# The narrow product's copy and lower part given out as scheduler steps, and a tile's first fifth-block product moved behind the fifth of the seven products

## The chip, the cores and the metric

One NeuronCore of a Trainium2 chip runs the program; the other cores are idle. The metric is the device time of one execution in microseconds (us). A kernel is run several times, and medians are compared. Times from the profile are from one profiled execution.

## What is computed

A layer with two residual parts over 4096 tokens of 640 channels. The first part is a spectral mixer: layer norm with a modulation from `c`, a two-dimensional FFT over the tokens, a complex two-layer MLP in four blocks of 160 channels with a soft shrink, and the inverse FFT. The second is a SwiGLU feed-forward network (FFN) with 1728 hidden channels. The change lies in the second.

```python
mod = (_silu(c) @ w_mod).reshape(c.shape[0], 6, 1, -1)
sa, ca, ga, sb, cb, gb = (mod[:, 0], mod[:, 1], mod[:, 2], mod[:, 3], mod[:, 4], mod[:, 5])
h = _layernorm(x, axis=-1) * (1 + ca) + sa
x = x + ga * _A_ref(h, A_w1, A_b1, A_w2, A_b2)
h = _layernorm(x, axis=-1) * (1 + cb) + sb
x = x + gb * _B_ref(h, B_w_gate, B_w_up, B_w_down)
...
g = _silu(x @ w_gate)
u = x @ w_up
return (g * u) @ w_down
```

All data is fp32. `_B_ref` is the FFN; `x` has 4096 rows of 640, `w_gate` and `w_up` are 640 by 1728, `w_down` is 1728 by 640.

## The kernel before

**Numbers.** Every fp32 operand is split in a high part (rounded to the type fp32r, which TensorE multiplies) and a low part (the rest). A product is three matmuls: high weight by high activation, high weight by low activation, low weight by high activation. In the code these are three lines next to each other, such as L1996, L1997, L1998.

**Tiles.** The FFN takes the tokens in six tiles. Tiles 0 and 1 have 512 tokens and use the plain form (`plain`). Tiles 2 to 5 have two halves of 384 tokens and use a form with seven products of half-size blocks in place of eight (`seven`, L1961): the 640 input channels are four blocks of 128, on which the seven products B11, B21, T3, T2, T4, T1 and B22 work, and a fifth block, which is multiplied in the ordinary way (`fifth`, three matmuls at L2007 to L2009). Each of the seven is six matmuls. The weights B are columns of the weight tile `wb`, the weights T are sums of them in `wt`. The eight activation operands of a tile, `h_0` to `h_7`, come from DRAM (`hs`) by two DMAs of SyncE's (SP's) queue each (`load_h`, L1808); `h_3` is the fifth block.

**Blocks of hidden channels.** 1728 channels are 13.5 blocks of 128. The first index `n` of `seven` is the block: a gate block and an up block of weights come in turn, `g0, u0, s, g1, u1, ...`. The entry `s` is the narrow remainder of 64 gate and 64 up columns, done after the first two blocks: inline in `plain` for tiles 0 and 1, by `rest` (L2125, matmuls L2160) for tiles 2 to 5, where it has two pieces, `a` = 0 and 1. What follows the matmuls of a narrow product is `mix_rem` (L1884): ScalarE (ACT) takes the silu of the gate rows (L1887), VectorE (DVE) multiplies by the up rows (L1888), ACT copies the result to the high part (L1889), DVE subtracts it for the low part (L1890). The result `a13` is read by the last down product of the tile.

**Banks.** The seven products accumulate in four banks of PSUM (the `1` in `pw_0_1` is the bank of that product). `keep` (L2015) copies a bank to SBUF on ACT (`s_x`, `s_v`, `s_y`, `s_z`), after which PE goes on to accumulate in the same bank, so that the second use of bank 0, for T2, waits for `s_x`. `summed` (L2022) adds bank and copy on DVE and gives the bank free. `lefts` makes the seven left factors `L_j` of the down product from the results: multiplications and differences on GpSimd (POOL, L2056 and L2067), high parts on ACT (L2072), low parts on DVE (L2076).

**What sets the order.** PE's stream is written by hand. Work of the other engines is of two kinds. Inline work is issued where it stands, so that it has its place in its engine's queue at that point of PE's stream. The rest are chains of steps (`Chain`, `Step`), each with an engine, an estimated cost, the keys it depends on, the key it gives and the buffers that it uses and frees. Between matmuls, `slot` moves a planner's clock on and issues the steps whose engines are free by the estimates, chains of the list `tails` first. `quiet` keeps steps off ACT just before a `keep`, `until` issues steps until a key is there, `hold` and `take` get a buffer. Each engine, and SP's queue of DMAs, works through its own queue in order, and SP's DMA waits for the one eight DMAs earlier. So the planner's estimates fix an order, and a change of one step's kind or cost can move those that come after it: residual rows (`cr`, `x`, stored as `x2d`, L1603 to L1662), transposes (`pt`), the second transform of the mixer for later rows (`py`, L1636), weights (`prep_w`: high part on ACT at L1383, low part on DVE at L1390), weights of the down product (`wq`, L1565). The down products' results are `pc` and `pe` (L2293, L2336).

Of the kernel before, what the change touches and what calls it, by code (L numbers as in the profile page):

```python
# [8 lines left out]
AF = mybir.ActivationFunctionType  # L9
OP = mybir.AluOpType  # L10
# [163 lines left out]
def body(tc, x, w1, b1, w2, b2, wg, wu, wd, c, wm, k_fa, k_tb, k_tx, k_bm, k_bx, k_ga, k_ge, k_id, out, dbg=None):  # L174
    nc = tc.nc
    pe, act, dve, pool = nc.tensor, nc.scalar, nc.vector, nc.gpsimd
    mm = pe.matmul

    def f32(ap):
        return ap.bitcast(F32)  # L180
# [21 lines left out]
    with ExitStack() as top:  # L202
# [836 lines left out]
        with ExitStack() as ff:  # L1039
# [203 lines left out]
            def core(e, n, at=0.0):  # L1243
                start = max(free[e], now[0] + 0.17, at)
                free[e] = start + n
                return free[e] + LAT
# [634 lines left out]
                done["fv"] = 5.0  # L1881
                return pg

            def mix_rem(pg, n, a13, nm, tag="sg"):  # L1884
                hold(tag)
                sg = take(tag, [P, n], F32, 4, f"sgr{nm}")
                act.activation(sg[0:64], pg[0:64, :n], AF.Silu)  # L1887
                dve.tensor_tensor(sg[0:64], pg[64:128, :n], sg[0:64], op=OP.mult)  # L1888
                act.activation(a13[0:64, :], sg[0:64], AF.Copy)  # L1889
                dve.tensor_tensor(a13[64:128, :], sg[0:64], f32(a13[0:64, :]), op=OP.subtract)  # L1890
                x = core("A", n / 960 + 0.09)
                x = core("V", n / 960 + 0.15, x)
                x = core("A", n / 960 + 0.09, x)
                x = core("V", n / 960 + 0.15, x)
                room[tag].append(x)
                return x


            def plain(t, n):
                k, p = WG[n]  # L1900
                wb = wbs[t, n]
                pg = []
                for f in range(1 if k == "s" else 2):
                    if (t, n) == (0, 0):
                        if f == 0:
                            hold("p1")
                            b2 = first_g()
                            slot(7.4)
                        pg.append((b2[f], "p1" if f else None))
                    else:  # L1910
                        b, q = any_bank(f"pg{t}_{n}_{f}")
                        pg.append((b, q))
                        for kk in range(5):
                            if t:
                                until(("ht", t, kk))
                                wait_pe(done["ht", t, kk])
                            hh, hl = (ht[t, kk][:, i] for i in range(2))
                            wh, wl = (wb[:, i, kk, 128 * f:128 * f + 128] for i in range(2))
                            mm(b, wh, hh, start=(kk == 0), stop=False)  # L1919
                            mm(b, wh, hl, start=False, stop=False)  # L1920
                            mm(b, wl, hh, start=False, stop=(kk == 4))  # L1921
                            if n == NW - 1 and f == 1:
                                room[f"h{HT0[kk]}"].append(now[0] + 0.9)
                            slot(0.68)
                    if k == "s":
                        hold("rb0")
                        a13 = take("rb0", [P, 512], F32R, 1, f"a13_{t}")
                        acts[t, 13] = (a13, a13)
                        x = done["act", t, 13] = mix_rem(b, 512, a13, f"{t}")
                    else:  # L1930
                        x = finish0(t, n, f, pg[f][0])
                    if pg[f][1]:
                        room[pg[f][1]].append(x)
# [27 lines left out]
            def seven(t, n, last):  # L1961
# [41 lines left out]
                def fifth(q, half, f):  # L2003
                    need_h(3)
                    AK = hb[t, 3]
                    c = slice(P * f, P * f + P)
                    mm(bk[q], wb[:, 0, 4, c], AK[:, half, 0], start=False, stop=False, skip_group_check=True)  # L2007
                    mm(bk[q], wb[:, 0, 4, c], AK[:, half, 1], start=False, stop=False, skip_group_check=True)  # L2008
                    mm(bk[q], wb[:, 1, 4, c], AK[:, half, 0], start=False, stop=True, skip_group_check=True)  # L2009
                    go(3)  # L2010

                def keep(q, nm):
                    hold("s")
                    s = take("s", [P, N], F32, 10, f"s{t}_{n}_{nm}")
                    act.activation(s, bk[q], AF.Copy)  # L2015
                    return s, core("A", ca_)
# [79 lines left out]
                def rel(q, at):  # L2096
                    room[f"p{q}"].append(at)
# [8 lines left out]
                s1 = keep(0, "x")  # L2106
                quiet[0] = now[0] + 5 * m3
                prod(1, 1, "B21", True)
                fifth(1, 0, 0)
                rel(1, summed(0, 0, 1, s1))  # L2110
                need_wt(0)
                prod(3, 6, "T3", True)
                s7 = keep(3, "v")
# [7 lines left out]
                prod(0, 4, "T1")  # L2121
                room[wtags[t, n, 1]].append(now[0] + 0.2)
                sz = keep(0, "z")
                fifth(3, 1, 0)
                rel(3, summed(1, 0, 3, sy))  # L2125
                quiet[0] = now[0] + 5 * m3
# [10 lines left out]
            def rest(t, n):  # L2137
                N = P * TL[t][1]
                wb = wbs[t, n]
                A11, A12, A22, AK, S1 = (hb[t, j] for j in range(5))  # L2140
                for key in wb_keys(t, n):
                    until(key)
                    wait_pe(done[key])
                for a in range(2):
                    b, q = any_bank(f"pr{t}_{a}")
                    b = b[:, :N]
                    seq = []
                    for kp in range(2):
                        c = slice(0, P)
                        w1_ = [wb[:, hl, kp, c] for hl in range(2)]  # L2150
                        if a == 0:
                            w2_ = [wb[:, hl, 2 + kp, c] for hl in range(2)]
                        else:
                            w2_ = [wb[:, hl, kp, P:256] for hl in range(2)]
                        for l, w in (((A11, S1)[a], w1_), ((A12, A22)[a], w2_)):
                            seq += [(w[0], l[:, kp, 0]), (w[0], l[:, kp, 1]), (w[1], l[:, kp, 0])]
                    w = [wb[:, hl, 4, 0:P] for hl in range(2)]
                    seq += [(w[0], AK[:, a, 0]), (w[0], AK[:, a, 1]), (w[1], AK[:, a, 0])]
                    for i, (l, m) in enumerate(seq):
                        mm(b, l, m, start=(i == 0), stop=(i == len(seq) - 1))  # L2160
                        if i % 5 == 4:
                            slot((N + 32) / 2400 * 5)
                    hold("s")
                    a13 = take("s", [P, N], F32R, 10, f"a13_{t}_{a}")
                    acts.setdefault((t, 13), {})[a] = a13
                    x = done["act", t, 13, a] = mix_rem(b, N, a13, f"{t}_{a}", "s")
                    room[q].append(x)

            def down(t, pp):
# [311 lines left out]
```

## Time and profile before

| what | value |
|---|---|
| time, three runs | 1432.89, 1424.74, 1430.14 us |
| median of the three | 1430.14 us |
| the profiled execution's own time | 1433.04 us |
| its span in the trace | 1431.2 us |
| mean granted TensorE clock | 0.995 |
| the FFN's part of the span | from about 317 us to the end |

The profile gives for each engine the busy time, and for groups of instructions what ended the idle time before them (the releaser). An instruction that waits for several things is put down to the one that came last. In a timeline row stand the start, the duration, the engine, the line, the operation and, in brackets, the idle time before it with the releaser; `xN` at the end is a row of N instructions alike.

### The profile page before, as it was taken

The page shows a single profiled execution, that of the slowest core. Times are in us where ns is not written, and L with a number is a line of the kernel's source. Part 1 is how long each engine was busy: PE and PEld are TensorE (multiplying, and loading weights), DVE is VectorE, ACT ScalarE, POOL GpSimd, SP SyncE. Part 2 cuts the span into 40 slices and gives each one's busy share as a digit, 9 for nine tenths or more (in the row PEclk, how much of TensorE's full clock was granted, in tenths as well). Part 3 has the DMA queues.
Part 4 walks back from the last instruction along what each step waited for, and adds up shares of the span by engine and source line. Part 5 has one row for each costly group of instructions (what it writes and reads, how often), then busy time and mean ns, then how long its engine had stood idle before and what let it go on. Part 6 is the DMA issues. An engine that isn't in the chain of part 4 may idle for free.

```text
span 1431.2 us, 23776 instructions
## 1 busy us (share of the span) xinstructions
PE 1392.4 (97%) x8410; PEld 1313.5 (92%) x8410; DVE 1055.1 (74%) x1863; ACT 762.7 (53%) x1542; POOL 595.5 (42%) x681
## 2 busy tenths in 40 slices
PE   6899999999999999999999999999999999999999
PEld 2599999967888888899999999999999999999998
DVE  8979888879987797738787669787667557365654
ACT  6879999736555556435463446445355325152441
POOL 5600200036767586325455426456433325052241
PEclk9999999989999999999999999999999999999999
DMA  9866556556889988898868998888988566955634
GB/s 361 319 221 199 164 184 197 188 201 210 314 290 317 344 301 306 290 353 307 307 206 296 343 348 280 270 276 293 373 304 296 185 216 246 365 189 198 217 124 147
DMA packets 170872, 377.34 MB, mean 264 GB/s; under 512 B 22177, under 2 KB 81633, under 8 KB 168738
## 3 DMA queue, kind: packets, MB, share of 16 engines
q1 hardware_dynamic: 161650, 359.28, 72.9%
q0 software_dynamic: 6800, 13.93, 3.0%
q10 hardware_dynamic: 2304, 2.62, 0.5%
q8 instruction: 66, 1.08, 0.3%
q14 instruction: 52, 0.43, 0.1%
HBM read 269.48 MB, written 96.80 MB: 256 GB/s over the span
## 4 chain that ended last, share of the span: by engine, by line
PE 65%; issue 9%; DVE 9%; DMA 7%; ACT 5%; POOL 3%; SPq 1%; POOLq 0%; DVEq 0%; ACTq 0%
PE pc L2293 8%; PE pw L1996 7%; PE pw L1998 7%; PE pw L1997 7%; PE pe L2293 6%; PE pd L2209 5%; PE pg L1920 3%; PE pg L1919 3%; PE pg L1921 3%; PE pw L2007 2%; PE pw L2009 2%; PE pw L2008 2%; DMA h<-hs 2%; PE py L1636 1%; DVE wb L1390 1%
## 5 line engine op out<-in xcount | busy, mean ns | idle before, releaser
L1390 DVE TENSOR_TENSOR wb<-r,wb 128x768 fp32r<-128x768 f32 (+3 forms) x170 | 158.8, 947 | 14.3 <-ACT wb L1383 13.7
L2056 POOL TENSOR_TENSOR sg<-s_x,sg 128x384 f32<-128x384 f32 x24 | 30.3, 1261 | 278.9 <-DVE s_x L2022 278.9
L1996 PE MATMUL pw<-h,wt 128*128 128x384 f32 x412 | 139.8, 339 | 3.8 <-ACT s_x L2015 2.9
L1998 PE MATMUL pw<-h,wt 128*128 128x384 f32 x412 | 138.3, 336 | 0.0
L1997 PE MATMUL pw<-h,wt 128*128 128x384 f32 x412 | 138.1, 335 | 0.0
L2293 PE MATMUL pc<-wq,L 128*128 128x320 f32 x846 | 132.8, 310 | 2.5 <-DVE s_v L2022 1.7
L1383 ACT ACTIVATE wb<-r 128x768 fp32r<-128x768 f32 (+3 forms) x168 | 104.2, 638 | 53.3 <-PE pw L2009 38.8
L2293 PEld LDWEIGHTS pc<-wq,L 128*128 128x128 f32 x846 | 126.3, 188 | 3.3 <-DVE s_v L2022 2.2
L2015 ACT ACTIVATE s_x<-pw 128x384 f32<-128x384 f32 x52 | 25.5, 490 | 190.6 <-PE pw L1998 188.4
L2076 DVE TENSOR_TENSOR L<-sg,L 128x384 fp32r<-128x384 f32 x144 | 101.2, 720 | 27.8 <-ACT L L2072 26.8
L1996 PE MATMUL pw<-h,wb 128*128 128x384 f32 x312 | 104.9, 336 | 0.0
L1997 PE MATMUL pw<-h,wb 128*128 128x384 f32 x312 | 104.4, 335 | 0.0
L1998 PE MATMUL pw<-h,wb 128*128 128x384 f32 x312 | 104.3, 334 | 0.0
L1919 PE MATMUL pg<-ht,wb 128*128 128x512 f32 x260 | 102.1, 393 | 0.0
L1920 PE MATMUL pg<-ht,wb 128*128 128x512 f32 x260 | 101.3, 390 | 0.0
L1921 PE MATMUL pg<-ht,wb 128*128 128x512 f32 x260 | 101.3, 390 | 0.0
L2293 PE MATMUL pe<-wq,L 128*128 128x320 f32 x648 | 101.0, 309 | 0.0
L2209 PE MATMUL pd<-wq,a 128*128 128x320 f32 x632 | 97.0, 310 | 0.0
L2293 PEld LDWEIGHTS pe<-wq,L 128*128 128x128 f32 x648 | 96.5, 188 | 0.0
L2067 POOL TENSOR_TENSOR sg<-sg,sg 128x384 f32<-128x384 f32 x72 | 88.3, 1227 | 18.7 <-DVE L L2076 15.5
L2209 PEld LDWEIGHTS pd<-wq,a 128*128 128x128 f32 x632 | 93.4, 188 | 0.5
L2250 DVE TENSOR_TENSOR x<-x,pc 128x320 f32<-128x320 f32 x144 | 68.2, 483 | 31.5 <-PE pc L2293 31.2
(317 smaller groups left out, 3865.4 us busy)
## 6 DMA issues: line engine op xcount, KB each, us to landing
wq<-wqd SPq DMA_DIRECT2D x83, 640.0 KB, 5.3
wt<-td SPq DMA_DIRECT2D x103, 512.0 KB, 4.8
hs<-ho SPq DMA_DIRECT2D x52, 512.0 KB, 5.9
h<-hs SPq DMA_DIRECT2D x32, 768.0 KB, 7.7
td<-wt SPq DMA_DIRECT2D x25, 512.0 KB, 6.4
r<-in_B_w_gate_dram SPq DMA_DIRECT2D x24, 384.0 KB, 4.8
r<-in_B_w_up_dram SPq DMA_DIRECT2D x24, 384.0 KB, 4.1
xx<-tt SPq DMA_DIRECT2D x56, 160.0 KB, 3.3
```

The source lines that it names most:

```text
L1383: def high(ks, e=slice(0, c), copy=lambda o, i: act.activation(o, i, AF.Copy)):
L1390: dve.tensor_tensor(wbs[t, n][:, 1, ks, e], raw[t, n][:, ks, e], f32(wbs[t, n][:, 0, ks, e]), op=OP.subtract)
L1919: mm(b, wh, hh, start=(kk == 0), stop=False)
L1920: mm(b, wh, hl, start=False, stop=False)
L1921: mm(b, wl, hh, start=False, stop=(kk == 4))
L1996: mm(b, w(0, kp), a[:, kp, 0], start=start and kp == 0, stop=False, skip_group_check=not start)
L1997: mm(b, w(0, kp), a[:, kp, 1], start=False, stop=False, skip_group_check=not start)
L1998: mm(b, w(1, kp), a[:, kp, 0], start=False, stop=kp == 1, skip_group_check=not start)
L2067: pool.tensor_tensor(o, x, y, op=op)
L2076: dve.tensor_tensor(o[:, 1], raws[j], f32(o[:, 0]), op=OP.subtract)
L2209: mm(b[:, :320], l, m, start=start and i == 0, stop=stop and i == len(s) - 1)
L2293: mm(o[:, :320], ls[q][:, x, k], w[:, q, y], start=start and q == 0 and n == 0, stop=q == 1 and n == 2, skip_group_check=not start)
```

## The change

Two edits. First, in `mix_rem` the ACT copy and the DVE subtraction are no longer issued inline behind the multiplication. They become a chain of two steps in `tails`, with the key of the finished part passed in. The planner books the silu and the multiplication only, the function returns the end of the multiplication, and with that the product's PSUM bank is noted as free (in `rest` through `room[q]`); the buffer of `sgr` is freed by the second step. This concerns ten narrow products: one in each of tiles 0 and 1, two in each of tiles 2 to 5. Second, in `seven`, for the first block alone (`n == 0`, one place in each of tiles 2 to 5), the first fifth-block product and the addition that frees its bank move from behind B21 to behind T1 and the copy `s_z`: four products, or 24 matmuls, later.

```diff
@@ -1881,18 +1881,18 @@
                 done["fv"] = 5.0
                 return pg
 
-            def mix_rem(pg, n, a13, nm, tag="sg"):
+            def mix_rem(pg, n, a13, key, nm, tag="sg"):
                 hold(tag)
                 sg = take(tag, [P, n], F32, 4, f"sgr{nm}")
                 act.activation(sg[0:64], pg[0:64, :n], AF.Silu)
                 dve.tensor_tensor(sg[0:64], pg[64:128, :n], sg[0:64], op=OP.mult)
-                act.activation(a13[0:64, :], sg[0:64], AF.Copy)
-                dve.tensor_tensor(a13[64:128, :], sg[0:64], f32(a13[0:64, :]), op=OP.subtract)
                 x = core("A", n / 960 + 0.09)
                 x = core("V", n / 960 + 0.15, x)
-                x = core("A", n / 960 + 0.09, x)
-                x = core("V", n / 960 + 0.15, x)
-                room[tag].append(x)
+                done["mul", key] = x
+                tails.append(Chain([
+                    Step("A", n / 960 + 0.12, lambda: act.activation(a13[0:64, :], sg[0:64], AF.Copy), (("mul", key),), ("ah", key)),
+                    Step("V", n / 960 + 0.22, lambda: dve.tensor_tensor(a13[64:128, :], sg[0:64], f32(a13[0:64, :]), op=OP.subtract),
+                         (("ah", key),), key, free=(tag,))]))
                 return x
 
 
@@ -1926,7 +1926,7 @@
                         hold("rb0")
                         a13 = take("rb0", [P, 512], F32R, 1, f"a13_{t}")
                         acts[t, 13] = (a13, a13)
-                        x = done["act", t, 13] = mix_rem(b, 512, a13, f"{t}")
+                        x = mix_rem(b, 512, a13, ("act", t, 13), f"{t}")
                     else:
                         x = finish0(t, n, f, pg[f][0])
                     if pg[f][1]:
@@ -2106,8 +2106,9 @@
                 s1 = keep(0, "x")
                 quiet[0] = now[0] + 5 * m3
                 prod(1, 1, "B21", True)
-                fifth(1, 0, 0)
-                rel(1, summed(0, 0, 1, s1))
+                if n:
+                    fifth(1, 0, 0)
+                    rel(1, summed(0, 0, 1, s1))
                 need_wt(0)
                 prod(3, 6, "T3", True)
                 s7 = keep(3, "v")
@@ -2121,6 +2122,9 @@
                 prod(0, 4, "T1")
                 room[wtags[t, n, 1]].append(now[0] + 0.2)
                 sz = keep(0, "z")
+                if not n:
+                    fifth(1, 0, 0)
+                    rel(1, summed(0, 0, 1, s1))
                 fifth(3, 1, 0)
                 rel(3, summed(1, 0, 3, sy))
                 quiet[0] = now[0] + 5 * m3
@@ -2163,7 +2167,7 @@
                     hold("s")
                     a13 = take("s", [P, N], F32R, 10, f"a13_{t}_{a}")
                     acts.setdefault((t, 13), {})[a] = a13
-                    x = done["act", t, 13, a] = mix_rem(b, N, a13, f"{t}_{a}", "s")
+                    x = mix_rem(b, N, a13, ("act", t, 13, a), f"{t}_{a}", "s")
                     room[q].append(x)
 
             def down(t, pp):
```

The numbers of lines behind L2125 grow by 4. No instruction is added or removed. All engines' orders are the same up to the narrow product of tile 0, and differ in many places after it. Three places follow.

ACT in tile 3, from the first narrow piece (`pr_0`, result `a_3_0`) to the second (`pr_1`, `a_3_1`) and the copy `s_3_x` of the next block's first bank. Before:

```order
L1887 ACTIVATE sgr_0_9855<-pr_0_9825 64x384
L1889 ACTIVATE a_3_0_9854<-sgr_0_9855 64x384
L2072 ACTIVATE L_0_7_9882<-s_1_d 128x384
L2072 ACTIVATE L_0_2_9890<-sg_0_01_9672 128x384
L2072 ACTIVATE L_0_4_9893<-sg_0_11_9679 128x384
L1887 ACTIVATE sgr_1_9897<-pr_1_9860 64x384
L1889 ACTIVATE a_3_1_9896<-sgr_1_9897 64x384
L2015 ACTIVATE s_3_x<-pw_3_0_9902 128x384
L1383 ACTIVATE wb_4_9931<-r_4_9733 128x2x128
```

After:

```order
L1887 ACTIVATE sgr_0_9854<-pr_0_9814 64x384
L2072 ACTIVATE L_0_2_9863<-sg_0_01_9668 128x384
L2072 ACTIVATE L_0_4_9872<-sg_0_11_9673 128x384
L1893 ACTIVATE a_3_0_9853<-sgr_0_9854 64x384
L1383 ACTIVATE wb_3_9823<-r_3_9423 128x768
L1887 ACTIVATE sgr_1_9888<-pr_1_9857 64x384
L2072 ACTIVATE L_0_5_9897<-sg_0_10_9650 128x384
L1383 ACTIVATE wb_4_9903<-r_4_9706 128x2x128
L2015 ACTIVATE s_3_x<-pw_3_0_9892 128x384
L1893 ACTIVATE a_3_1_9887<-sgr_1_9888 64x384
```

The second narrow copy, which stood between the second silu and `s_3_x`, now stands behind `s_3_x`; the left factor `L_0_5` and a copy of the weights `wb_4` have come ahead of `s_3_x`, and the high part of the second piece of `wb_3` between the two silus.

DVE at the same place. Before:

```order
L1390 TENSOR_TENSOR wb_3_9835<-r_3_9423,wb_3_9835 128x2x128
L1390 TENSOR_TENSOR wb_3_9835<-r_3_9423,wb_3_9835 128x768
L1888 TENSOR_TENSOR sgr_0_9855<-pr_0_9825,sgr_0_9855 64x384
L1890 TENSOR_TENSOR a_3_0_9854<-sgr_0_9855,a_3_0_9854 64x384
L2076 TENSOR_TENSOR L_0_7_9882<-s_1_d,L_0_7_9882 128x384
L2076 TENSOR_TENSOR L_0_2_9890<-sg_0_01_9672,L_0_2_9890 128x384
L1888 TENSOR_TENSOR sgr_1_9897<-pr_1_9860,sgr_1_9897 64x384
L1890 TENSOR_TENSOR a_3_1_9896<-sgr_1_9897,a_3_1_9896 64x384
```

After:

```order
L1888 TENSOR_TENSOR sgr_0_9854<-pr_0_9814,sgr_0_9854 64x384
L2076 TENSOR_TENSOR L_0_2_9863<-sg_0_01_9668,L_0_2_9863 128x384
L2076 TENSOR_TENSOR L_0_4_9872<-sg_0_11_9673,L_0_4_9872 128x384
L1390 TENSOR_TENSOR wb_3_9823<-r_3_9423,wb_3_9823 128x2x128
L1888 TENSOR_TENSOR sgr_1_9888<-pr_1_9857,sgr_1_9888 64x384
L1390 TENSOR_TENSOR wb_3_9823<-r_3_9423,wb_3_9823 128x768
L1894 TENSOR_TENSOR a_3_0_9853<-sgr_0_9854,a_3_0_9853 64x384
```

The low parts of the next block's weights, `wb_3`, stood ahead of both narrow multiplications; now the second piece (128x768) stands behind the second multiplication.

SP in tile 4, from the loads of `wq` to those of `h_7` and `h_3` for its first `seven`. Before:

```order
L1565 DMA wq_2_0_11868<-wqt 128x1280
L1565 DMA wq_2_-1_11893<-wqt 128x1280
L1565 DMA wq_0_1_11913<-wqd 128x1280
L1808 DMA h_4_11927<-hs 128x1536
L1565 DMA wq_0_2_11932<-wqd 128x1280
L1808 DMA h_7_11943<-hs 128x1536
L1808 DMA h_3_11960<-hs 128x1536
L1744 DMA hs<-ho_1_0_11724 128x2x512
```

After:

```order
L1808 DMA h_2_11802<-hs 128x1536
L1565 DMA wq_2_-1_11824<-wqt 128x1280
L1607 DMA cr_11838<-s 128x640
L1662 DMA x2d<-x_11182 128x640
L1565 DMA wq_0_1_11864<-wqd 128x1280
L1808 DMA h_4_11886<-hs 128x1536
L1565 DMA wq_0_2_11891<-wqd 128x1280
L1662 DMA x2d<-x_11273 128x640
L1603 DMA x_11938<-in_A_x_dram 128x640
L1607 DMA cr_11954<-s 128x640
L1808 DMA h_7_11976<-hs 128x1536
L1808 DMA h_3_11998<-hs 128x1536
```

Two stores of rows, a load of a row and two loads of `cr` have come ahead of `h_7` and `h_3`. The row load (`x_11938`) waits, among other things, for the landing of the first of these stores.

## The prediction

> **What bounds the kernel now.** The page's head, with the busy time of each engine, and two stretches of the view of windows (us, then the busy time and instructions of PE, PEld, DVE, ACT and POOL, the granted TensorE clock, the DMA share, GB/s):
>
> ```profile
> span 1431.2 us, 23776 instructions
> PE 1392.4 (97%) x8410; PEld 1313.5 (92%) x8410; DVE 1055.1 (74%) x1863; ACT 762.7 (53%) x1542; POOL 595.5 (42%) x681
> ...
> 1030.00:1235.00 205.00, 203.41 (x1250) 202.40 (x1249) 128.49 (x234) 81.40 (x176) 66.01 (x63) 1.00 0.76 267
> 295.00:300.00 5.00, 4.80 (x13) 2.60 (x12) 4.89 (x8) 0.88 (x2) 0.31 (x1) 0.50 0.48 169
> ```
>
> TensorE sets the time, at the full clock (1.00) in the FFN's stretch; the other stretch lies before the FFN. The change neither adds nor removes a matmul, so it can only act on the moments in which PE waits. The view of waits, for PE in the FFN (317 us to the end), names these (engine, line, what it waited for: us in total, times, longest):
>
> ```profile
> PE pw L1996 <- ACT s_x L2015: 2.9, 3, 1.6
> PE py L1636 <- DVE chl L1626: 2.0, 2, 1.1
> PE pc L2293 <- DVE s_v L2022: 1.7, 2, 0.9
> PE py L1636 <- ACT a L1955: 1.6, 1, 1.6
> PE pw L2007 <- DMA h<-hs: 1.5, 2, 1.3
> PE pt L1699 <- ACT xn L1667: 1.2, 2, 0.8
> PE pw L1996 <- ACT s_v L2015: 0.8, 1, 0.8
> PE pc L2293 <- DMA wq<-wqd: 0.8, 1, 0.8
> PE pe L2336 <- DMA wq<-wqt: 0.4, 1, 0.4
> PE pt L1699 <- ACT h L1703: 0.2, 1, 0.2
> PE pt L1852 <- DVE xn L2379: 0.2, 1, 0.2
> ```
>
> They add up to 13.3 us, 0.9% of the span: the most that any reordering can bring. Two of the rows are what the change touches: 2.9 us on s_x, the copy of the first product's bank, and 1.5 us on h, the fifth block's activations. The other 8.9 us are at places that the edit doesn't name.
>
> **The narrow product's wait, in tile 3.** Rows of ACT, DVE, POOL and PE from the timeline (start, duration, engine, line; idle time before and its releaser in brackets):
>
> ```profile
> 856.83 1.02 POOL L2056 TENSOR_TENSOR sg<-s_v,sg 128x384 f32<-128x384 f32 x1
> 857.06 1.12 PE L2160 MATMUL pr<-h,wb 128*128 128x384 f32 x5
> 857.17 1.08 DVE L1890 TENSOR_TENSOR a<-sgr,a 64x384 fp32r<-64x384 f32 x1 [0.59 <-ACT a L1889]
> 858.02 0.33 PE L1996 MATMUL pw<-h,wb 128*128 128x384 f32 x1
> 858.31 0.47 ACT L1887 ACTIVATE sgr<-pr 64x384 f32<-64x384 f32 x1
> 859.06 0.33 PE L1996 MATMUL pw<-h,wb 128*128 128x384 f32 x1
> 860.03 1.36 DVE L2076 TENSOR_TENSOR L<-sg,L 128x384 fp32r<-128x384 f32 x1
> 861.31 0.55 DVE L1888 TENSOR_TENSOR sgr<-pr,sgr 64x384 f32<-64x384 f32 x1
> 861.90 0.52 ACT L1889 ACTIVATE a<-sgr 64x384 fp32r<-64x384 f32 x1 [3.12 <-DVE sgr L1888]
> 862.33 0.47 ACT L2015 ACTIVATE s_x<-pw 128x384 f32<-128x384 f32 x1
> 862.45 0.57 DVE L1890 TENSOR_TENSOR a<-sgr,a 64x384 fp32r<-64x384 f32 x1 [0.59 <-ACT a L1889]
> 862.85 0.45 PE L1996 MATMUL pw<-h,wt 128*128 128x384 f32 x1 [1.02 <-ACT s_x L2015]
> 867.38 0.95 DVE L1390 TENSOR_TENSOR wb<-r,wb 128x768 fp32r<-128x768 f32 x1
> ```
>
> ACT stood still 3.12 us before the narrow copy (L1889), because the multiplication (L1888) started only at 861.31, behind left factors on DVE. The copy of the first product's bank, s_x, was behind it in ACT's order, and PE needed that bank again. So the wait hangs on one instruction placed inline. The change takes it from that place, at ten places in all. The two first rows of the next fence are the same wait in tile 2 (651 to 657 us) and in tile 4 (1068 to 1073 us); the third row groups the low part at all ten (ns: min, median, max):
>
> ```profile
> PE pw L1996 <- ACT s_x L2015: 1.6, 1, 1.6
> ...
> PE pw L1996 <- ACT s_x L2015: 0.3, 1, 0.3
> ...
> L1890 DVE TENSOR_TENSOR a<-sgr,a x10: 552/742/1193, 343.9 to 1263.0; 64x384 fp32r<-64x384 f32 x8, 64x512 fp32r<-64x512 f32 x2
> ```
>
> **Its cost, step by step.** Removed: 1.6 in tile 2, 1.0 in tile 3, 0.3 in tile 4. But the order of the changed program shows something new in tile 3: on DVE, the second piece of the next weights' low part (128x768, 0.95 us in the row at 867.38) now stands behind the second multiplication, and that waits for the narrow product's end, which I call E. Ready is it at about E + 0.13 (858.31 less the end 858.18 of PE's row at 857.06) + 0.47 (silu) + 0.55 + 0.95 and some 0.1 of handovers, E + 2.2. PE gets to B21's first matmul with the low weights after the six of B11 (858.02 to 859.06: 1.04 us, 0.173 each) and two more, at E + 1.4. So PE waits 0.8 us there, and of tile 3's 1.0 remain 0.2. On ACT, s_x has the left factor L_5 and a weight copy ahead of it now; PE uses the bank again 15 matmuls after B11, 2.6 us, and 0.8 more with that wait, which covers both. Sum: -1.6 - 1.0 + 0.8 - 0.3 = -2.1 us. Bounds: -2.9, if the low weights come in time; 0, if each stall only goes over to the next item in ACT's and DVE's orders. I take -2.1, since of the three places the order shows a new wait at one.
>
> The copies and low parts themselves (10 of 0.52 us, 10 of 0.55 to 1.19) are done later, beside matmuls on engines that are busy 53% and 74% of the span; only the last down products of a tile read them, tens of us later. Were that cover gone, the longest pair would be 0.52 + 1.19 = 1.7 us at one place. Cost taken: 0.
>
> **The fifth block's product.** PE in tiles 3 and 4 (timeline), the piece before it from the chain that ended last, SP's issues of h_7 and h_3, and landing times grouped by issue (KB, median us), for h between 1000 and 1045 us and for the row store between 590 and 630:
>
> ```profile
> 833.77 0.44 PE L2007 MATMUL pw<-h,wb 128*128 128x384 f32 x1 [0.21 <-DMA h<-hs]
> ...
> 1040.93 0.34 PE L1998 MATMUL pw<-h,wb 128*128 128x384 f32 x1
> 1042.61 0.44 PE L2007 MATMUL pw<-h,wb 128*128 128x384 f32 x1 [1.34 <-DMA h<-hs]
> ...
> 1031.38 11.19 DMA h<-hs
> ...
> 1025.11 0.34 SPq L1565 DMA_DIRECT2D wq_-1_11893<-wqt  x1
> 1030.76 1.05 SPq L1808 DMA_DIRECT2D h<-hs  x2
> ...
> h<-hs SPq DMA_DIRECT2D x8, 768.0 KB, 9.0
> ...
> x2d<-x SPq DMA_DIRECT2D x2, 320.0 KB, 9.6
> ```
>
> Four products now stand ahead of the matmul that waits: 4 x 1.04 = 4.2 us. In tile 3 SP's order around the loads is unchanged, so the 0.2 goes. In tile 4 the matmul would be reached at 1041.10 + 4.17 = 1045.3 (1041.10 is 1040.93 and one pitch). With h_3 landing at 1042.57 as before (1031.38 + 11.19) the 1.3 would be gone. But in the changed order h_7 and h_3 stand behind two row stores, a row load and two loads of cr. The row load waits for the landing of the first store, which stands right behind the wq issue at 1025.11, so it starts at about 1025.8. By the landing of 9.6 the load is let go at 1035.4; it and cr take some 0.9 us of SP by the issue rows (0.34 to 0.5 each), so h_7 and h_3 go out at about 1036.3 and 1036.8, 5.5 us later than now. Landing takes 9.0 by the median of that stretch (1045.8, a wait of 0.5) to 11.19 (1048.0, a wait of 2.7). Against 1.34 now that is -0.8 to +1.4, and -1.3 if the store lands early. I take a wait of 0.9, near the median: -0.4.
>
> The bank of the moved product is held 4.2 us longer. Its next use (B21 of the next block) comes 21 matmuls behind the fifth, 3.6 us, and the addition that frees it is one pass of DVE, which has 37% of that stretch free: 0. The silu behind it is read only by the next block's multiplications: 0.
>
> **Everything else moves too.** From tile 0's narrow product on, rows, transposes, weights and left factors stand elsewhere in all engines' orders. The 8.9 us of waits not aimed at are dealt anew. Nothing in the trace tells the sign: 0, bounds -8.9 and +8.9.
>
> Sum: -2.1 - 0.2 - 0.4 = -2.7. The profiled execution took 1433.04 us, its span of 1431.2 and 1.8 around it; 1433.0 - 2.7 = 1430.3. That execution lies 2.9 above the median of the three runs (1430.14), so for a median I say 1427.4, rounded **1427**.
>
> **Rivals.**
>
> (1) *Stalls only change places.* ACT and DVE work in order; taking one item out lets the stall go to the next. For it: the new 0.8 us in tile 3. Against it: tiles 2 and 4 show no new producer in that place. Time: 1430.
>
> (2) *The full gain.* The waits aimed at go (4.4), and the new order also drops half or more of the 8.9. For it: freeing ACT's head of line helps any item behind it, ACT's idle 3.12 us among them. Against it: nothing names those waits. 1430.1 - 4.4 - 4.5 = 1421; at most 1417.
>
> (3) *Loads come late behind row stores: slower.* In tile 4 the order puts a load that waits for a store's landing ahead of h_7 and h_3, and SP is a queue in order. My price there is at worst +1.4. If the same pattern leaves one whole landing (9.6) uncovered at a further place, in h, weights or the reload of rows, the sum is -2.1 - 0.2 + 1.4 + 9.6 = +8.7: 1439. It decides once PE waits on DMA some 10 us more than the 2.7 it does now. For it: the order, and landings up to 11.19. Against it: the DMA share is 0.76 in the window from 1030 on, so not every landing there should be that long.
>
> The granted clock is 0.50 in the stretch from 295 us and 1.00 in the FFN's, whose longest wait is 1.6. The Trainium skill, "TensorE: Matmul & The Clock Gate", Part 1: The HAM clock gate, says that TensorE falls to half its clock after an idle window of about 3.4 us. The trace agrees as far as it goes: no wait of the FFN is that long. By that page a landing left uncovered would cost one more such window at half speed, an estimated 1.7 us on top of rival 3.
>
> (4) *Low parts collide with POOL: the gain is used up.* The low part at 857.17 took 1.08 us while POOL's multiplication at 856.83 ran, the one at 862.45 took 0.57 with none of it beside. In the new order the low parts stand among POOL's left factors. Ten times at most 1.19 - 0.55 = 6.4 us on DVE; DVE is 74% busy, so perhaps half shows on PE: 1427 + 3 = 1430. Against it: median 742 ns, so a part of them collides already.
>
> The Trainium skill, "SBUF — State Buffer", Who interferes with whom, states such a rule: a DVE instruction with two SBUF inputs and a GpSimd instruction that reads SBUF exclude each other for its whole length. The two rows agree with it.
>
> **How the numbers follow.** A difference under 0.5% (7.2 us) can't be told from no change here. Forecast 1427: chance 0.40. Rival 1: 0.17. Rival 4: 0.06. These three lie within 0.5% (0.63; with tails 0.60). Rival 2: 0.18, and 0.14 of it and 0.04 of the forecast's tail fall below 1423.0: faster 0.18. Rival 3: 0.19; with a tail of the reordering, slower (above 1437.3) 0.22. The range takes in rival 2's 1421 and most of the way to rival 3: 1419 to 1438.5. The forecast's own range, by the bounds of its terms (-2.9 - 0.2 - 1.3 and 0 - 0.2 + 1.4) and some 3 us of reordering, is 1423 to 1434.
>
> **What would show it.** In the changed profile's waits: s_x gone in tiles 2 and 4; in tile 3 a wait of about 0.8 us in B21 for the low weights (L1390); no h wait in tile 3, one of 0 to 2.7 in tile 4, now four products later; the other waits near 8.9 in sum. PE's busy time stays at 1392. I'm wrong if waits on DMA grow by over 5 us, if the sum of FFN waits falls below 6, or if s_x still waits over 1 us anywhere.

## The result, and the profile after

| | median | runs | ratio to before, 95% interval |
|---|---|---|---|
| before | 1429.50 us | 20 | |
| changed | 1433.82 us | 20 | 1.0032 [1.0023, 1.0042] |

The change made the kernel 4.3 us (0.3%) slower, where 2.7 us faster was forecast. The time lies in the predicted range, and within the 0.5% that was called no change, but on the other side. The profiled execution took 1435.42 us. The head of its page, then the waits of PE in the FFN (317 us to the end; us in total, times, longest):

```profile
span 1433.6 us, 23774 instructions
PE 1392.7 (97%) x8410; PEld 1314.1 (92%) x8410; DVE 1068.5 (75%) x1863; ACT 763.7 (53%) x1542; POOL 601.1 (42%) x681
```

```profile
PE py L1636 <- DVE chl L1626: 6.2, 5, 2.7
PE pe L2297 <- DVE s_v L2022: 1.7, 1, 1.7
PE pc L2297 <- DVE s_v L2022: 1.4, 1, 1.4
PE pt L1699 <- ACT xn L1667: 1.2, 1, 1.2
PE pw L1996 <- ACT s_y L2015: 0.9, 1, 0.9
PE pw L1998 <- DVE wb L1390: 0.7, 1, 0.7
PE pt L1699 <- ACT h L1703: 0.7, 1, 0.7
PE pw L1996 <- ACT s_v L2015: 0.6, 2, 0.4
PE pd L2213 <- DVE a L1956: 0.6, 1, 0.6
PE pg L1921 <- DVE wb L1390: 0.5, 1, 0.5
PE py L1636 <- ACT h L1703: 0.5, 1, 0.5
PE py L1636 <- DMA gt<-in_k_ga_dram: 0.4, 1, 0.4
PE pw L1996 <- ACT s_x L2015: 0.2, 1, 0.2
PE pt L1852 <- DVE xn L2383: 0.2, 1, 0.2
```

What the edits aimed at is gone: s_x fell from 2.9 to 0.2 us, the wait on h from 1.5 to nothing. The one new wait that was read off the order came as well, 0.7 us for the low weights (L1998 on L1390). The other waits rose from 8.9 us to 14.9: their row on chl alone went from 2.0 to 6.2. The sum of all is 15.8 us against 13.3, so 2.5 us more.

The largest single wait is in tile 0. Rows of DVE, POOL and PE there:

```profile
369.95 0.31 PE L1636 MATMUL py<-chh,gt 128*128 128x320 f32 x1
369.96 0.83 DVE L1390 TENSOR_TENSOR wb<-r,wb 128x512 fp32r<-128x512 f32 x1
370.20 4.08 POOL L1491 TENSOR_TENSOR wdr<-wdr,gbb 128x640 f32<-128x640 f32 x2
370.71 2.15 DVE L1626 TENSOR_TENSOR chl<-cr,chh 128x640 fp32r<-128x640 f32 x1
372.92 0.41 PE L1636 MATMUL py<-chl,gt 128*128 128x320 f32 x1 [2.66 <-DVE chl L1626]
```

PE began the transform of a row (py) with its high part and then waited 2.66 us for the low part, chl. That had another lower part ahead of it on DVE and took 2.15 us, beside a POOL multiplication that had begun 0.5 us earlier.

A second loss stands in no wait. Windows of both kernels, before the FFN and, for the changed one, around this wait (the third number from the end is the granted TensorE clock). Of before:

```profile
292.00:308.00 16.00, 14.58 (x37) 9.21 (x38) 10.21 (x17) 2.95 (x7) 0.54 (x1) 0.68 0.58 182
```

Of the changed kernel:

```profile
292.00:308.00 16.00, 14.94 (x44) 9.27 (x45) 11.27 (x18) 2.80 (x7) 2.21 (x3) 0.79 0.62 190
371.00:381.00 10.00, 8.08 (x44) 8.09 (x45) 9.88 (x17) 1.04 (x2) 6.70 (x6) 0.83 0.77 246
```

Just behind the wait of 2.66 us the clock fell: 10 x (1 - 0.83) = 1.7 us of full-speed time were lost. In the same way the dip before the FFN cost 16 x 0.32 = 5.1 us in this execution of before and 16 x 0.21 = 3.4 in that of the changed kernel. So the two spans are accounted for: waits +2.5, clock in the FFN +1.7, clock before it -1.7, together +2.5, measured 1433.6 - 1431.2 = 2.4. The dip before the FFN lies ahead of the first place at which the orders differ and varies from one execution to the next (the traces of fifth_only and late_both, whose order is the same there, have a clock of 1.00); without it the difference is 4.2 us, close to that of the medians (4.3). Each trace is one execution, but the clock's part can also be seen in the runs: its mean over the 20 runs of the changed kernel was 0.9957, over the 86 runs of before beside the experiments 0.9968, and 0.0011 of 1434 us are 1.6.

### The profile page after: what moved, and what is told of

It is laid out like the page before. It is cut to its first block, busy times and chain, and to the rows that moved or that the text cites. A ratio compares the mean times of both kernels' runs of the same rounds, so it can differ in the third digit from the quotient of the medians.

```text
span 1433.6 us, 23774 instructions
## 1 busy us (share of the span) xinstructions
PE 1392.7 (97%) x8410; PEld 1314.1 (92%) x8410; DVE 1068.5 (75%) x1863; ACT 763.7 (53%) x1542; POOL 601.1 (42%) x681
## 4 chain that ended last, share of the span: by engine, by line
PE 73%; issue 9%; DVE 7%; DMA 4%; ACT 3%; POOL 3%; SPq 1%; DVEq 0%; POOLq 0%; ACTq 0%
PE pc L2297 9%; PE pw L1996 8%; PE pw L1998 8%; PE pw L1997 8%; PE pe L2297 7%; PE pd L2213 6%; PE pg L1921 3%; PE pg L1920 3%; PE pg L1919 3%; PE pw L2009 2%; PE pw L2007 2%; PE pw L2008 2%; PE py L1636 2%; PE pc L707 1%; PE pl L657 1%
## 5 line engine op out<-in xcount | busy, mean ns | idle before, releaser
L1390 DVE TENSOR_TENSOR wb<-r,wb 128x768 fp32r<-128x768 f32 (+3 forms) x170 | 157.7, 937 | 16.1 <-ACT wb L1383 15.7
L1998 PE MATMUL pw<-h,wt 128*128 128x384 f32 x412 | 138.3, 336 | 0.0
L1998 PE MATMUL pw<-h,wb 128*128 128x384 f32 x312 | 104.5, 335 | 0.7 <-DVE wb L1390 0.7
L2067 POOL TENSOR_TENSOR sg<-sg,sg 128x384 f32<-128x384 f32 x72 | 92.2, 1281 | 15.3 <-DVE L L2076 12.1
L764 POOL DMA_DIRECT2D s<-co x28 | 15.6, 556 | 180.5 <-ACT co L763 180.5
```

The source lines that it names most:

```text
L1390: dve.tensor_tensor(wbs[t, n][:, 1, ks, e], raw[t, n][:, ks, e], f32(wbs[t, n][:, 0, ks, e]), op=OP.subtract)
L1998: mm(b, w(1, kp), a[:, kp, 0], start=False, stop=kp == 1, skip_group_check=not start)
L2067: pool.tensor_tensor(o, x, y, op=op)
```

## The experiments

All ratios are to runs of before on the same chip, whose medians were 1429.1 to 1430.2 us.

| kernel | median | ratio, 95% interval | PE's waits in one trace up to 600 us / behind it |
|---|---|---|---|
| before | 1429.5 | | 5.0 / 8.3 |
| changed | 1433.82 | 1.0032 [1.0023, 1.0042] | 8.0 / 7.8 |
| tiles25: both edits in tiles 2 to 5 alone | 1426.49 | 0.9986 [0.9969, 1.0004] | 4.5 / 4.8 |
| tiles01: first edit in tiles 0 and 1 alone | 1435.04 | 1.0047 [1.0029, 1.0065] | 9.0 / 8.0 |
| fifth_only: second edit alone | 1433.35 | 1.0030 [1.0016, 1.0044] | 6.5 / 10.5 |
| mix_only: first edit alone | 1434.86 | 1.0047 [1.0032, 1.0062] | 7.7 / 5.3 |
| frozen_both: the second narrow copy and the fifth-block product moved, all else in the order of before | 1427.48 | 0.9982 [0.9968, 0.9995] | 5.4 / 5.4 |
| book01: only what the planner is told | 1439.13 | 1.0072 [1.0053, 1.0092] | 6.7 / 9.6 |
| nudge_gated: one estimate of before + 0.02 us | 1436.90 | 1.0051 [1.0033, 1.0070] | 6.4 / 8.6 |
| nudge_chl: another estimate of before + 0.02 us | 1430.22 | 1.0006 [0.9989, 1.0023] | 6.4 / 6.7 |
| late_both: frozen, copy further back | 1424.47 | 0.9969 [0.9954, 0.9984] | 4.6 / 5.2 |
| late_copies: the same without the second edit | 1425.57 | 0.9980 [0.9967, 0.9994] | 3.5 / 5.7 |
| swap: changed, two DVE rows exchanged | 1433.29 | 1.0024 [1.0010, 1.0038] | 7.3 / 6.0 |
| all_nudge: changed, one estimate + 0.02 us | 1440.59 | 1.0085 [1.0070, 1.0100] | 7.6 / 10.6 |

The waits are sums over the rows that the view of waits prints. Line numbers of some of these kernels are shifted by a few; the names tell what is meant.

Each sum is that of one execution. For nudge_gated and swap the traced execution was the fastest of its kernel (1431.41 and 1427.68 us), so it need not show what the median lost. How far such a sum varies by itself can be read from kernels with one order: up to 600 us before, tiles25, fifth_only, frozen_both, late_both and late_copies have the same order, and 3.5 to 6.5 us of waits. The changed kernel, tiles01, mix_only and all_nudge share another order up to there, and have 7.6 to 9.0; the two groups don't overlap.

### Where the loss sits: tiles25, tiles01, fifth_only, mix_only

`mix_rem` got an argument that chooses between steps and the inline form (issued and booked as in the kernel before); each kernel sets it by place and has the second edit or not.

```diff
-                        x = mix_rem(b, 512, a13, ("act", t, 13), f"{t}")
+                        x = mix_rem(b, 512, a13, ("act", t, 13), f"{t}", step=False)
```

> Both edits in tiles 2 to 5 alone; tiles 0 and 1 keep the copy and the lower part inline. Theory A (the edits gain what they aim at in tiles 2 to 5, and the loss of some 5 us sits in tiles 0 and 1, where the new steps deal the order anew): about 3 us faster than before, 1426 to 1427; waits of PE up to 600 us as before (about 5 us, none on chl over 1.2), s_x at most 0.3 us. Rival B (the steps themselves cost, wherever they stand): slower than before by 2 us or more. Rival C (any new order of this kernel is worse by some us): slower by 3 to 5 us, with new waits in tiles 2 to 5.

> The first edit in tiles 0 and 1 alone, tiles 2 to 5 and the fifth-block product as before. Theory A: slower than before by 4 to 6 us, with the waits of the changed kernel on chl before 600 us (2.7 and 1.3 us); behind that the waits on s_x and h come back in some form. Rival B: slower by 1 to 2 us (two of ten places). Rival C: slower by 3 to 5 us, but with waits spread over all tiles.

> The fifth-block product moved, the copies and lower parts inline everywhere. Theory A: the waits on h (1.5 us) go, those on s_x stay near 2.9; 1 to 1.5 us faster than before, 1428. Rival B (for this edit: the bank held 4.2 us longer makes a wait): a new wait on a sum or a bank behind the moved product, slower. Rival C: slower by 3 to 5 us in tiles 2 to 5.

> Copies and lower parts as steps at all ten places, the fifth-block product where it was. Theory A: as the changed kernel up to 600 us (waits on chl of 2.7 and 1.3 us), s_x gone, a wait on h of 1 to 2.5 us back in tile 4; 1433 to 1436. Rival B: the same total, but the loss in every tile. Rival C: 1433 with the loss anywhere.

tiles25 came out 2.6 us below before in the medians (its interval takes in 1, so the gain is not shown by itself), at the 1426 to 1427 expected; the order of tiles 0 and 1 is that of before there. tiles01 is slower by 5.9. Its row on chl up to 600 us, and the largest of these waits:

```profile
PE py L1636 <- DVE chl L1626: 6.5, 3, 4.2
...
370.76 0.42 PE L1636 MATMUL py<-chl,gt 128*128 128x320 f32 x1 [4.16 <-DVE chl L1626]
```

It is the place of the 2.66 us in the changed kernel. So by these two the new order in tiles 0 and 1 carries the loss, though no wait there was aimed at. mix_only agrees in its median (1433 to 1436 expected), and its h wait is back (1.6 us), but the waits of its single trace (13.0 in sum, no more than before) don't show the 5.8 us. A part is the clock: its mean was 0.9955 over the runs of mix_only and 0.9973 over those of before beside them, some 2.6 us. The rest stays open.

fifth_only missed: 1 to 1.5 us faster was expected, 4.2 slower came. The h waits did go. Its order is that of before up to 625 us, so the loss lies behind that; its longest wait, 2.87 us at 383 us, stands where the order is unchanged (before waited 1.65 us at the same product). In tile 3, PE's rows with waits:

```profile
855.00 0.45 PE L2006 MATMUL pw<-h,wb 128*128 128x384 f32 x1 [1.27 <-DVE wb L1390]
856.77 0.45 PE L2004 MATMUL pw<-h,wb 128*128 128x384 f32 x1 [0.79 <-ACT wb L1383]
857.82 0.44 PE L2006 MATMUL pw<-h,wb 128*128 128x384 f32 x1 [0.44 <-DVE wb L1390]
```

These are low and high weights that came late, at a place which the edit doesn't touch. No wait on the bank that is held longer appears. So rival C of these expectations holds for this one: a new order can lose in tiles 2 to 5 as well. The parts don't add up either: 5.8 and 4.2 make 4.3 together.

### Is it the edits or the order: frozen_both, book01, nudge_gated, nudge_chl

In frozen_both the planner books everything as in before; only the issue is put off: of the second narrow piece's copy and lower part until behind s_x, of the three matmuls, the addition and, where due, the silu until behind s_z. Against before, 12 matmuls (three in each tile), 6 instructions of ACT and 2 of DVE stand at another place, and none of SP and POOL.

```diff
+                if later:
+                    pend.append(halves_of)
+                else:
+                    halves_of()
...
                     act.activation(s, bk[q], AF.Copy)
+                    while pend:
+                        pend.pop()()
...
-                fifth(1, 0, 0)
-                rel(1, summed(0, 0, 1, s1))
+                if n:
+                    fifth(1, 0, 0)
+                    rel(1, summed(0, 0, 1, s1))
+                else:
+                    need_h(3)
+                    go(3)
+                    owed = []
+                    end1 = summed(0, 0, 1, s1, owed)
```

> Both edits in tiles 2 to 5 with the order of everything else frozen as before: the planner is told the old story, the second narrow piece's copy is issued behind s_x, the first block's fifth product four products later. If the aimed gains are real (theory A): s_x waits 2.9 to under 0.5 us, h waits 1.5 to 0, all other waits as before (8.9 us); 4 us faster than before, 1425. If stalls only change places (rival): the sum of PE's waits stays near 13, 1429.

It is faster than before by 2.7 us (0.18%, interval clear of 1), less than the 4 expected. s_x and h are gone from its waits, but s_v rose:

```profile
PE pw L2003 <- ACT s_v L2023: 2.8, 3, 1.1
...
652.83 0.52 ACT L1892 ACTIVATE a<-sgr 64x384 fp32r<-64x384 f32 x1 [1.52 <-DVE sgr L1890]
653.26 0.51 ACT L2087 ACTIVATE L<-sg 128x384 fp32r<-128x384 f32 x1
653.67 0.47 ACT L2023 ACTIVATE s_v<-pw 128x384 f32<-128x384 f32 x1
654.19 0.44 PE L2003 MATMUL pw<-h,wt 128*128 128x384 f32 x1 [0.99 <-ACT s_v L2023]
```

The copy, now behind s_x, still stood idle 1.52 us for its multiplication, and s_v behind it. The stall had gone to the next copy of a bank, as the rival has it, for 1.0 of the 4.4 us. The other two waits on s_v, 1.07 us at 940.47 and 0.75 at 1002.73, stand far from any narrow product (those of tile 3 begin at 848 us, of tile 4 at 1056), and the first of them was there before, with 0.81 us.

book01 keeps the copies inline and only tells the planner what the change tells it, in tiles 0 and 1. The nudges change one number of before.

```diff
+                if tag == "sg":
+                    room[tag].append(x + 0.5)
+                    return x
                 x = core("A", n / 960 + 0.09, x)
                 x = core("V", n / 960 + 0.15, x)
```

```diff
-                return ([Step("P", 1.62, gated, (k("cr"), "fv"), k("crg")),
+                return ([Step("P", 1.64, gated, (k("cr"), "fv"), k("crg")),
```

> Tiles 0 and 1 alone, and there only what the planner is told: the copy and lower part stay inline, but are not booked, and the bank counts as free at the end of the multiplication. If the loss in tiles 0 and 1 is that of a new order (theory A): slower than before by 2 to 6 us although no instruction was taken out of line, with new waits on chl. If it is the later copy itself that costs (rival): no slower than before, 1429.

> Before, with one estimate of the planner raised by 0.02 us (POOL's multiplication of a row, 1.62 to 1.64), which deals the order anew without any purpose. If a new order alone moves the time by several us (theory A): 2 us or more away from before, to the slow side more likely than not. Rival (orders are all alike, the steps cost): within 1 us of before.

> Before, with another estimate raised by 0.02 us (DVE's lower part of a row, 0.83 to 0.85). It moves fewer instructions. Theory A: 0 to 4 us away from before, either sign, with the difference in the waits of PE where the order differs. Rival: within 1 us.

book01 lost 9 us with nothing taken out of line, and nudge_gated 6.7 us with no edit at all. In book01's trace the clock is at half for four stretches of 3.4 us in the FFN, at three waits (two of them in a row at the wait of 2.70 us): 4 x 1.7 = 6.8 us, more than the 3.0 that its waits grew. The runs agree: the mean clock was 0.9915 over those of book01 and 0.9965 over those of before beside them, 7.2 of the 9 us. Rows of book01, its two longest waits,

```profile
372.66 0.64 PE L1636 MATMUL py<-chl,gt 128*128 128x320 f32 x1 [3.78 <-DVE chl L1626]
...
837.26 0.69 PE L2010 MATMUL pw<-h,wb 128*128 128x384 f32 x1 [2.70 <-DMA h<-hs]
```

and of nudge_gated, with the windows behind it,

```profile
1038.94 0.58 PE L2007 MATMUL pw<-h,wb 128*128 128x384 f32 x1 [3.64 <-DMA h<-hs]
...
1038.00:1042.00 4.00, 3.06 (x10) 3.06 (x11) 0.56 (x1) 0.00 (x0) 0.00 (x0) 0.64 1.03 412
1042.00:1046.00 4.00, 4.00 (x23) 4.00 (x22) 0.76 (x2) 2.04 (x6) 0.00 (x0) 0.94 0.80 257
```

nudge_chl, which moves far fewer instructions, made no difference that the interval shows (its single trace has the s_x waits at 1.2 and other waits in their place). A new order alone cost 0 to 9 us in these three, and was never a gain; three are few.

### Cleaner, and at one place: late_both, late_copies, swap, all_nudge

late_both issues the put-off copies behind s_z in place of s_x; late_copies leaves out the second edit. swap exchanges the two DVE neighbours shown above, and nothing else in any order.

```diff
-                    while pend:
+                    while nm == "z" and pend:
                         pend.pop()()
```

```diff
                 def low(ks, e=slice(0, c)):
+                    if (t, n) == (0, 7) and not swapped:
+                        swapped.append(lambda: low(ks, e))
+                        return
...
                     dve.tensor_tensor(chs[r][1], crs[r], f32(chs[r][0]), op=OP.subtract)
+                    if r == 6:
+                        swapped[0]()
```

> As the frozen kernel with both edits, but the second narrow copy is issued behind s_z, three bank copies later than s_x. In the frozen kernel s_v waited 2.8 us (0.8 before), since the copy, still waiting for its multiplication, stood ahead of s_v on ACT. If that is the cause: s_v back to about 0.8, s_x near 0, h at 0; 4 to 5 us faster than before, 1425. Rival (the wait goes on to s_y or s_z): as the frozen kernel, 1427.5.

> The same without the fifth-block product's move: only four copies and four lower parts stand elsewhere than before. If the terms of the sum add up: s_x gone, h still 1.5 us; 2.5 to 3 us faster than before, and 1.5 slower than the kernel with both edits. Rival: no difference between the two, when the h wait is taken up by another transfer.

> The changed kernel with one pair of neighbours on DVE exchanged: the lower part of row 6 (chl) ahead of the lower part of a weight (128x512), on which nothing waits there. In the changed kernel PE waited 2.7 us for that chl, which took 2.15 us beside a POOL multiplication begun 0.5 us ahead of it. If the wait is a matter of DVE's order alone: 0.8 us less. If the collision with POOL is most of it, and the earlier start avoids it: 1.5 to 2 us less. Rival (PE waits for something else there, such as the row's other operands): no change. In the total: 0.8 to 2 us faster than the changed kernel, 1432 to 1433.

> The changed kernel with one estimate of the planner raised by 0.02 us (POOL's multiplication of a row, 1.62 to 1.64). If the loss belongs to the new order and not to the edits (theory A): 1 us or more away from the changed kernel, either sign. If the edits themselves cost the 4 us: within 1 us of it.

late_both is 0.31% faster than before, 1424.47 us, and beats both kernels. Its waits behind 600 us begin with

```profile
PE pc L2320 <- DVE s_v L2033: 1.7, 2, 0.9
PE pw L2003 <- ACT s_v L2023: 1.5, 2, 0.7
PE pt L1699 <- ACT xn L1667: 0.7, 1, 0.7
PE pw L2003 <- ACT s_y L2023: 0.7, 1, 0.7
```

with no s_x and no h. The s_v row fell from 2.8 to 1.5 only. PE's rows with these waits:

```profile
935.64 0.45 PE L2003 MATMUL pw<-h,wt 128*128 128x384 f32 x1 [0.71 <-ACT s_v L2023]
998.35 0.45 PE L2003 MATMUL pw<-h,wt 128*128 128x384 f32 x1 [0.75 <-ACT s_v L2023]
1036.94 0.44 PE L2003 MATMUL pw<-h,wt 128*128 128x384 f32 x1 [0.68 <-ACT s_y L2023]
```

None is at a narrow product: the two on s_v are the two that frozen_both has there as well, and the one at the narrow product of tile 2 is gone. So putting the copy further back did what it was meant to. The expectation had put 2.0 of the 2.8 us down to the copy, where 1.0 was due to it. The wait on s_y is in the first block of tile 4, where the second edit stands; late_copies, without that edit, waits for h there. late_copies lies between before and late_both, 3.7 us faster than before (2.5 to 3 expected), and its h wait is 1.1 us; the step from it to late_both (1.1 us, intervals overlapping) is the second edit's term as far as it can be told.

swap, at the exchanged place:

```profile
365.26 0.96 DVE L1631 TENSOR_TENSOR chl<-cr,chh 128x640 fp32r<-128x640 f32 x1
365.50 2.15 POOL L1496 TENSOR_TENSOR wdr<-wdr,gbb 128x640 f32<-128x640 f32 x1
366.14 2.06 DVE L1395 TENSOR_TENSOR wb<-r,wb 128x512 fp32r<-128x512 f32 x1
366.28 0.42 PE L1643 MATMUL py<-chl,gt 128*128 128x320 f32 x1 [0.73 <-DVE chl L1631]
```

chl, begun ahead of POOL's multiplication, took 0.96 us in place of 2.15, and PE waited 0.73 in place of 2.66: 1.9 us less at this place, where the order alone gives 0.8. The weight's lower part now met the POOL instruction and took 2.06 in place of 0.83. Up to 600 us the waits on chl fell by 1.1 us only (4.0 against 5.1), since others followed. In the total, 0.5 us in the medians and intervals that overlap: the trace shows the mechanism at its place, the times don't tell it apart.

all_nudge is 6.8 us slower than the changed kernel, for 0.02 us in one estimate. Its order is that of the changed kernel up to 978 us; behind that, waits of 2.42 us on s_z and 2.38 us on a weight are new. The edits are the same in both.

## Why the prediction was wrong

**The aimed terms came out, one of them by luck.** The narrow product: -2.1 was forecast; s_x fell by 2.7 and the new wait in tile 3 took 0.72 (0.8 forecast), -2.0. Its parts held: tiles 2 and 4 clean, tile 3 with the low weights behind the second multiplication. The fifth-block product: -0.6 forecast, -1.5 measured. In tile 4, h_7 and h_3 did go out behind the row load, at 1037.65 where 1036.3 was worked out. But PE came to that tile 4.65 us later than before (its first product at 1043.65 against 1039.00). SP's row of the two loads, the time to landing of the second, h_3, and the matmul that reads it:

```profile
1037.65 1.01 SPq L1808 DMA_DIRECT2D h<-hs  x2
...
h<-hs SPq DMA_DIRECT2D x1, 768.0 KB, 11.4
...
1049.91 0.35 PE L2007 MATMUL pw<-h,wb 128*128 128x384 f32 x1
```

Issued at 1038.2, h_3 landed at 1049.6, 0.3 us ahead of the matmul. At the 1045.3 that the prediction worked out for this matmul it would have waited 2.5 to 4.3 us (an estimate; the less if the loads, whose queue was 1.8 us later than before at the wq issue ahead of them, had gone out that much earlier). So in tile 4 the missing wait is luck: the loss elsewhere had made PE late. The 0.2 us of tile 3 went as said. That the bank held longer costs nothing held too.

**The step that failed** is "Everything else moves too ... Nothing in the trace tells the sign: 0". Those 8.9 us became 14.9, +6.0, half of it before 600 us, in tiles 0 and 1. The bounds (8.9 either way) held it, the centre did not. That the centre belongs on the slow side is what nudge_gated, nudge_chl and book01 point to: orders dealt anew at the same work came out level or 7 to 9 us slower, and all_nudge lost 6.8 us to the changed kernel. It would fit that the order of before is a good one by its own waits, 13.3 us or 1.2% of the FFN, so that a new one has more to lose than to gain; that is an argument and was not tested. A second part of it was left out: the sum counted waits at face value, and rival 3 gave the clock's cost only to a wait of 9.6 us. A wait of 2.66 us brought 1.7 us on top. Together -2.0 - 1.5 + 6.0 + 1.7 = +4.2. The prediction's signs of being wrong (waits on DMA, a sum below 6, s_x over 1 us) had none for this and none of them came; what failed of the things to be seen was other waits near 8.9. And a difference under 0.5% can be told here: with 20 runs of each kernel the interval reaches 0.1% to either side.

**The rivals.** Rival 3 had the right sign for the wrong cause: waits on DMA in the FFN fell from 2.7 us to 0.4. Rival 1 is true of the ACT copies in part (frozen_both, 1.0 of 4.4 us), but it ends at no change and not at slower. Rival 2 would have needed the others to fall. Rival 4 named the right resource at the wrong instructions: the moved lower parts got no dearer (median 618 ns where it was 742), and nobody waited for them; it was another lower part, chl, that met POOL's multiplication ahead of a waiting PE.

**What settles it.** With the rest of the order frozen the two edits gain 2.7 us, and 4.7 with the copy further back; the first is done there for the second narrow piece of tiles 2 to 5 alone, which is the one that s_x had waited behind. With the order free they lose 4.3. Copies of tiles 0 and 1 taken out of line with the order frozen were not run; what speaks against a cost of their own is book01, which lost 9 us with all copies inline.

## What to carry to other kernels

Where a planner sets the order, an edit is two edits: the one meant and a new deal of everything behind it. Try it first with the planner's books left as they were and only the issue put off; if that gains and the free order loses, keep the frozen form, or look for a better deal with the edit in it. When a deal is new, don't set its centre at zero: run the old kernel with one estimate nudged and see what a new order costs by itself.

## What the runs showed of the hardware

A wait of PE of over 2 us can cost more than itself. In the traces of all these kernels the FFN has twelve waits of 2.0 to 4.2 us. During or just behind eight of them the granted clock fell (those of 2.66 us in the changed kernel, 4.16 in tiles01 and 3.64 in nudge_gated among them, the shortest 2.1 in book01), as a rule for about 1.7 us of full-speed time: 0.83 in a window of 10 us, and 0.50 from 374 to 376 us in the changed kernel. At four it did not (2.9 us in fifth_only, 2.68 and 2.42 in all_nudge, 2.0 in book01), nor at any wait up to 1.9 us. The Trainium skill, "TensorE: Matmul & The Clock Gate", Part 1: The HAM clock gate, says that TensorE is at half its clock after at least one idle window of about 3.4 us, and that this window runs freely. By that page's figure one window at half speed loses an estimated 1.7 us, which fits, but the traces have the loss from 2.1 us of wait on, and the measurement decides.

The spread of one kernel's runs goes with the clock: of the changed kernel's 20 runs the fastest, 1429.92 us, had a mean of 0.999 and the slowest, 1436.84, of 0.994; 0.005 of 1434 us are 7.2, and the two lie 6.9 apart. It is not all of it: over the 20 runs time and clock have a correlation of -0.79.

A DVE instruction can be held up by one of POOL: chl took 2.15 us when POOL's 128x640 multiplication had begun before it and 0.96 when it began first. The other way round is not shown: that multiplication took 2.15 us behind chl in swap, and 1.5 to 2.3 us over the 28 of its kind in the changed kernel. The Trainium skill, "SBUF — State Buffer", Who interferes with whom, says that a DVE instruction with two SBUF inputs contends with a GpSimd instruction that reads SBUF, for ports that are an exclusive lock, and that the order of issue decides who blocks; for DVE, swap agrees.
